# A decode kernel for two attentions: part of B's wo on eight DMA engines, wo rows permuted over partitions, finer last loads, x loaded first

## The chip, the cores and the metric

The kernel runs on one core of a Trainium2 chip. The metric is the device time in microseconds (us); the kernel before takes 254.8 us. The span of a profile is about 2 us shorter than that time.

In the profile lines, PE is TensorE (matmuls), DVE is VectorE, ACT is ScalarE, POOL is GpSimd and SP is SyncE, which issues the big loads; a q behind a name marks the engine's queue, and L500 is line 500 of that kernel. A semaphore is a counter on which engines wait.

## The reference, cut to what matters

Two independent attentions with one query row each, A over a window of the last 2048 cache rows, B over all 8192.

```python
D = 576; Hq, Hkv, Sk, Dh = 32, 16, 8192, 128        # bf16; wo: (Hq*Dh, D) = (4096, 576)
q = (x @ wq).reshape(1, 1, Hq, Dh)                  # for A and for B
k, v = k_cache[:, :, Sk - W:], v_cache[:, :, Sk - W:]   # A: W = 2048; B: all rows
p = softmax(q @ k^T * Dh**-0.5)                     # two query heads share one kv head
out = (p @ v).reshape(1, 1, Hq * Dh) @ wo           # (1, 1, 576) each, concatenated
```

Nothing is used twice, so some 103 MB have to be read once. Of these, the two wo matrices are 2 x 4096 x 576 x 2 B = 9.4 MB.

## The kernel before

All big loads come from one queue (SP) and go through six buffers (slots) of 128 partitions x 16 KB. The recording helper `add` lists operations with the resources that they read and write and makes the semaphore waits from that.

```python
    def load(src_of, view_of, what):
        s = slot_n[0] % NSLOT
        slot_n[0] += 1
        res = ("slot", s)
        add("sp", lambda sp: sp.dma_start(view_of(slots[:, s, :]), src_of()), writes=[res], dma="slot%d" % s)
        return s
    # ... (cut)
    def load_wo(P, k):                       # WO_SLOT = 14: three loads of 14, 14 and 4 rows per partition
        lo, hi = k * WO_SLOT, min(HQ, (k + 1) * WO_SLOT)
        return load(lambda: wos[P].rearrange("(p j) n -> p (j n)", p=128)[:, lo * DM:hi * DM],
                    lambda v: v[:, 0:(hi - lo) * DM], "wo")
```

Partition p holds rows 32p to 32p+31 of wo; "row 14" below means row 14 of these 32 on every partition. The attention result is brought into the same layout (`opj`) by matmuls with a 0/1 matrix `pick`; then each of the 32 rows takes four matmuls, one for each quarter of the 576 columns.

```python
    for j in range(4):
        add("pool", select(pick[:], -128 * j, [[1, 4], [-1, 128]], 4), reads=["pick"], writes=["pick"])
    # ... (cut)
    for jj in range(lo, hi):                 # in wo_part
        for j in range(4):
            o = (jj - lo) * DM + j * OUTW
            ins = pe.matmul(misc[32 * j:32 * j + 32, 0:OUTW], lhsT=opj[:, P, jj:jj + 32],
                            rhs=slots[:, s, o:o + OUTW], start=(jj == 0), stop=(jj == HQ - 1))
    # ... (cut) the end of the kernel
    for k in range(3):
        wo_part(0, k, load_wo(0, k))
    finish_out(0)
    vb1 = list(range(NS[1]))
    v_some(1, 1, vb1, NS[1])                 # the last eight V loads of B
    store_out(0)
    combine(1)
    for k in range(3):
        wo_part(1, k, load_wo(1, k))
    finish_out(1)
    store_out(1)
```

## Time and profile before

| what | before |
|---|---|
| time, median of 4 runs | 254.83 us |
| span of the profile | 252.8 us |
| DMA: mean rate over the span | 408 GB/s |
| last wo load landed, eight fastest engines / last engine | 242.8-244.1 / 249.3 us |
| matmuls left when B's second wo load had landed | 72, from 247.95 to 250.3 us |

The busy share in 40 slices (each 6.3 us, digits are tenths) and the rate of the DMA in each slice, kernel before:

```profile
DMA  7999999999999999999999999999999999999960
GB/s 283 398 440 430 433 415 428 433 417 425 432 423 423 430 423 423 433 421 423 430 417 436 425 415 436 430 412 441 421 421 419 430 425 425 428 423 429 425 284 31
```

The DMA engines are busy for nine tenths or more of every slice from the second to the 38th. The kernel is bound by the stream of loads.

The table of DMA queues before (queue, kind: packets, MB, share of the time of 16 engines):

```profile
q1 hardware_dynamic: 7504, 102.77, 96.1%
q8 instruction: 27, 0.44, 0.7%
```

The second line is the fetching of the program itself, in 27 packets of 16 KB.

The trace also records every increment of a semaphore by a DMA. A load of 128 partitions leaves 16 such landings, and the page counts 16 DMA engines, so each landing is read here as the end of that load on one engine. They are not a view of the profile page; here they are read from the trace, sorted by time within one load, in us from the start of the span:

```
before, the third K load of A: 28.6 to 29.1 on all sixteen
before, last load of B's wo (rows 28-31):
  242.83 242.84 242.90 243.00 243.05 243.43 243.71 244.14
  247.35 247.37 247.42 247.46 247.56 247.63 249.06 249.30
```

Sixteen engines that started together end in two groups of eight. The fast eight got a 2 MB load done every 4.89 us throughout. The others fell back in steps of about 1.45 us. There were 26 instruction fetches by then (a median of 1.07 us each); spread over eight engines in turn that would give six engines three and two engines four of them, which fits the two groups within the late eight. The trace fits it all the way: at the loads that landed first at 64, 128, 182 and 222 us, the late eight were 5, 13, 19 and 24 such steps behind in sum, and 5, 13, 19 and 24 fetches had begun. Below, "early" and "late" engines mean these.

The tail before, in order of time (start us, us, engine, line, operation, [idle before it and what ended that]):

```profile
243.44 1.87 PE L500 MATMUL misc<-slots,opj 128*32 128x144 bf16 x56 [0.37 <-DVE opj L491]
247.95 2.35 PE L500 MATMUL misc<-slots,opj 128*32 128x144 bf16 x72 [2.64 <-DMA slots<-in_B_wo_dram]
250.36 0.31 DVE L506 CAST outsb<-misc 128x144 bf16<-128x144 f32 x1 [7.06 <-PE misc L500]
250.69 0.58 SPq L512 DMA_DIRECT2D out_dram<-outsb  x1
```

PE does the first 14 rows (56 matmuls) at once, waits for the second load, and then has 72 matmuls left.

### The profile page before, as it was taken

The numbers are of one execution on the slowest core, as the hardware profiler recorded it, in microseconds if no ns is written. First come the engines' busy times: TensorE is split into PE (matmuls) and PEld (weight loads), VectorE is DVE, ScalarE is ACT, GpSimd is POOL, SyncE is SP. The second block draws the span as 40 slices with busy tenths as digits, with TensorE's granted clock in tenths as the row PEclk, the third lists the DMA queues.
The fourth block names the chain that finished last, engine by engine and source line by source line (L and its number), as shares of the span: only waits on it lengthen the run. The fifth ranks groups of instructions, "written<-read, shape, count | busy, mean of one in ns | idle before, by whom it ended". The sixth has DMA issues, their size and how long they took to land.

```text
span 252.8 us, 7319 instructions
## 1 busy us (share of the span) xinstructions
PE 167.1 (66%) x3438; PEld 131.7 (52%) x3438; DVE 79.3 (31%) x141; ACT 87.3 (35%) x92; POOL 22.4 (9%) x31
## 2 busy tenths in 40 slices
PE   0018999787799995888694994858943634332563
PEld 0003877456578874766474673655732633232453
DVE  0181545427544462357341340313425100000010
ACT  2000766445566683565461461423630000000000
POOL 8996000000000000000000000000000000000000
PEclk9999999999979999799997798968977665555555
DMA  7999999999999999999999999999999999999960
GB/s 283 398 440 430 433 415 428 433 417 425 432 423 423 430 423 423 433 421 423 430 417 436 425 415 436 430 412 441 421 421 419 430 425 425 428 423 429 425 284 31
DMA packets 7822, 103.24 MB, mean 408 GB/s; under 512 B 1136, under 2 KB 1136, under 8 KB 1648
## 3 DMA queue, kind: packets, MB, share of 16 engines
q1 hardware_dynamic: 7504, 102.77, 96.1%
q8 instruction: 27, 0.44, 0.7%
q10 hardware_dynamic: 288, 0.00, 0.1%
q14 instruction: 3, 0.02, 0.0%
HBM read 102.76 MB, written 0.00 MB: 407 GB/s over the span
## 4 chain that ended last, share of the span: by engine, by line
DMA 53%; PE 38%; DVE 6%; issue 1%; POOL 1%; ACT 0%; SPq 0%; POOLq 0%
DMA slots<-in_B_k_cache_dram 21%; PE ktps L339 20%; DMA slots<-in_B_v_cache_dram 17%; DMA slots<-in_B_wo_dram 11%; PE sacc L362 7%; DMA xtwo<-in_A_x_dram 4%; PE opsum L464 3%; DVE xpad L287 3%; PE opsum L302 2%; PE misc L302 2%; PE misc L500 2%; DVE ptm L407 1%; PE misc L396 1%; PE misc L444 1%; PE misc L431 0%
## 5 line engine op out<-in xcount | busy, mean ns | idle before, releaser
L345 ACT ACTIVATE kt<-ktps 128x1024 bf16<-128x1024 bf16 x80 | 78.0, 1023 | 65.3 <-PE ktps L339 65.1
L339 PE MATMUL ktps<-ident,slots 128*128 128x128 bf16 x1280 | 86.4, 231 | 19.1 <-DMA slots<-in_B_k_cache_dram 19.1
L339 PEld LDWEIGHTS ktps<-ident,slots 128*128 128x128 bf16 x1280 | 80.0, 105 | 31.5 <-DMA slots<-in_B_k_cache_dram 20.3
L348 DVE COPY kt<-ktps 128x1024 bf16<-128x1024 bf16 x80 | 55.3, 691 | 79.2 <-PE ktps L339 79.0
L464 PE MATMUL opsum<-slots,ptm 128*32 128x128 bf16 x1280 | 28.3, 256 | 29.4 <-DMA slots<-in_B_v_cache_dram 28.9
L464 PEld LDWEIGHTS opsum<-slots,ptm 128*32 128x32 bf16 x1280 | 24.5, 116 | 35.6 <-DMA slots<-in_B_v_cache_dram 33.0
L362 PE MATMUL sacc<-kt,qtm 128*32 128x512 bf16 (+1 forms) x384 | 30.1, 411 | 0.3 <-DVE kt L348 0.3
L302 PE MATMUL opsum<-slots,xpad 128*32 128x512 bf16 x72 | 8.7, 460 | 19.3 <-DVE xpad L287 19.3
L302 PEld LDWEIGHTS opsum<-slots,xpad 128*32 128x32 bf16 x72 | 2.5, 112 | 22.2 <-issue 21.3
L224 POOL MEMSET ptm<- 128x8192 uint32 x2 | 13.8, 6926 | 0.0
L478 DVE TENSOR_SCALAR acc<-opsum,stat 128x128 f32<-128x128 f32 x2 | 0.7, 346 | 39.6 <-PE opsum L464 39.6
L362 PEld LDWEIGHTS sacc<-kt,qtm 128*32 128x32 bf16 x384 | 7.0, 98 | 6.9 <-ACT kt L345 1.1
L500 PE MATMUL misc<-slots,opj 128*32 128x144 bf16 x256 | 8.1, 323 | 3.4 <-DMA slots<-in_B_wo_dram 2.6
L308 ACT ACTIVATE qrow<-opsum 128x512 bf16<-128x512 f32 x2 | 1.2, 597 | 24.1 <-PE misc L302 24.1
L500 PEld LDWEIGHTS misc<-slots,opj 128*32 128x32 bf16 x256 | 7.4, 146 | 3.8 <-DMA slots<-in_B_wo_dram 3.4
L287 DVE TENSOR_SCALAR xpad<-xtwo,par 128x5 bf16<-128x5 bf16 x4 | 6.4, 3098 | 8.3 <-DMA xtwo<-in_A_x_dram 8.3
L302 PE MATMUL misc<-slots,xpad 128*32 128x512 bf16 x72 | 8.5, 450 | 0.0
L385 ACT ACTIVATE psb<-sacc,stat 128x2048 bf16<-128x2048 f32 x3 | 5.9, 1967 | 7.5 <-DVE stat L379 7.5
L562 POOL MEMSET ptm<- 128x512 uint32 x1 | 0.5, 526 | 86.1 <-PE opsum L464 86.1
L407 DVE TENSOR_SCALAR ptm<-misc,par 128x256 bf16<-128x256 bf16 (+1 forms) x16 | 6.9, 526 | 3.7 <-PE misc L396 3.7
L396 PE MATMUL misc<-ident,psb 128*128 128x128 bf16 x48 | 4.1, 235 | 3.7 <-DVE ptm L407 3.7
L396 PEld LDWEIGHTS misc<-ident,psb 128*128 128x128 bf16 x48 | 3.0, 105 | 5.4 <-DVE ptm L407 4.3
(50 smaller groups left out, 37.2 us busy)
## 6 DMA issues: line engine op xcount, KB each, us to landing
slots<-in_B_k_cache_dram SPq DMA_DIRECT2D x16, 2048.0 KB, 22.3
slots<-in_B_v_cache_dram SPq DMA_DIRECT2D x16, 2048.0 KB, 25.1
slots<-in_A_k_cache_dram SPq DMA_DIRECT2D x4, 2048.0 KB, 19.3
slots<-in_A_v_cache_dram SPq DMA_DIRECT2D x4, 2048.0 KB, 20.7
slots<-in_A_wq_dram SPq DMA_DIRECT2D x2, 2048.0 KB, 9.6
slots<-in_B_wq_dram SPq DMA_DIRECT2D x2, 2048.0 KB, 18.6
slots<-in_A_wo_dram SPq DMA_DIRECT2D x2, 2016.0 KB, 25.0
slots<-in_B_wo_dram SPq DMA_DIRECT2D x2, 2016.0 KB, 28.7
```

What stands on the lines that cost most here:

```text
L224: add("pool", lambda pool, b=b: pool.memset(ptm[:, b, :].bitcast(U32), 0), writes=[("ptm", b)])
L287: add("dve", lambda dve, e=e: dve.tensor_scalar(xpad[:, P, 5 * e:5 * e + 5, 0], xtwo[:, P, 0:5], par[2][:, e:e + 1], None, ALU.mult), read ...
L302: ins = pe.matmul(qps[c][32 * j:32 * j + 32, :], lhsT=xpad[:, P, x, :], rhs=slots[:, s, o:o + 512], start=(u == 0), stop=(u == WQ_UNITS - 1))
L339: ins = pe.matmul(ktps_bf[q][:, t * 128:(t + 1) * 128], lhsT=slots[:, s, o:o + 128], rhs=ident[:, :], start=True, stop=True, is_transpose= ...
L345: add("act", lambda act, q=q, dst=dst: act.activation(dst, ktps_bf[q], ACT.Copy), reads=[("bank", q)], writes=[("kt", u, q)])
L348: add("dve", lambda dve, q=q, dst=dst: dve.tensor_copy(dst, ktps_bf[q]), reads=[("bank", q)], writes=[("kt", u, q)])
L362: ins = pe.matmul(sacc[32 * j:32 * j + 32, o:o + w], lhsT=qtm[:, P, g * 32:(g + 1) * 32], rhs=rhs, start=(g == 0 and o % 512 == 0), stop=( ...
L385: return act.activation(psb[:, 0:w * G[P]].rearrange("p (x g) -> p x g", g=G[P]), src, ACT.Exp, bias=st(P, C_NB + c), scale=SCALE, accum_o ...
L396: ins = pe.matmul(misc_bf[:, t * 128:(t + 1) * 128], lhsT=psb[:, o:o + 128], rhs=ident[:, :], start=True, stop=True, is_transpose=True)
L407: ins = dve.tensor_scalar(dst, src, par[G[P]][:, e:e + 1], None, ALU.mult)
L464: ins = pe.matmul(opsum[32 * j:32 * j + 32, 0:DH], lhsT=ptm[:, pb, o:o + 32], rhs=slots[:, s, b * 128:(b + 1) * 128], start=(i == 0 and u ...
L500: ins = pe.matmul(misc[32 * j:32 * j + 32, 0:OUTW], lhsT=opj[:, P, jj:jj + 32], rhs=slots[:, s, o:o + OUTW], start=(jj == 0), stop=(jj == ...
```

## The change

The intent was to let the eight early engines take over some of the late engines' load, to leave less PE work behind the last landing, and to start PE earlier. Rows 14-19 of B's wo go in two halves of 64 partitions, whose source pattern has an outermost dimension of 8. For that, the rows are permuted over the partitions (partition 8a+b holds row block a+16b), for A and B alike. The last four rows go in two loads of two. x is loaded first, and the memset of ptm (the buffer for the transposed softmax weights, cleared by POOL at the start) is cut into pieces. Two tiny probe loads were left in.

```diff
-        return load(lambda: wos[P].rearrange("(p j) n -> p (j n)", p=128)[:, lo * DM:hi * DM],
-                    lambda v: v[:, 0:(hi - lo) * DM], "wo")
+    def load_wo(P, parts):
# ... (cut)
+            for h in range(2 if halves else 1):
+                p0, pn = (64 * h, 64) if halves else (0, 128)
+                def go(sp, p0=p0, pn=pn, lo=lo, n=n, o=o):
+                    src = bass.AP(tensor=wo.tensor, offset=wo.offset + (p0 // 8) * HQ * DM + lo * DM,
+                                  ap=[[HQ * DM, pn // 8], [16 * HQ * DM, 8], [1, n]])
+                    return sp.dma_start(slots[p0:p0 + pn, s, o:o + n], src)
# ... (cut)
-        add("pool", select(pick[:], -128 * j, [[1, 4], [-1, 128]], 4), reads=["pick"], writes=["pick"])
+        add("pool", select(pick[:], -128 * j, [[1, 4], [-1, 16], [-16, 8]], 4), reads=["pick"], writes=["pick"])
# ... (cut)
-    for k in range(3):
-        wo_part(0, k, load_wo(0, k))
+    for parts in ([(0, 14, 0)], [(14, 28, 0)], [(28, 32, 0)]):
+        for made in load_wo(0, parts):
+            wo_part(0, *made)
# ... (cut) two probe loads of 8 and 12 partitions, 512 B each
-    for k in range(3):
-        wo_part(1, k, load_wo(1, k))
+    for parts in ([(0, 14, 0)], [(14, 20, 1), (20, 28, 0)], [(28, 30, 0), (30, 32, 0)]):
+        for made in load_wo(1, parts):
+            wo_part(1, *made)
# ... (cut) load_x(0), load_x(1) moved to the head of ACT's queue
-        add("pool", lambda pool, b=b: pool.memset(ptm[:, b, :].bitcast(U32), 0), writes=[("ptm", b)])
+        for h in range(8):
+            add("pool", lambda pool, b=b, h=h: pool.memset(ptm[:, b, h * 2048:(h + 1) * 2048].bitcast(U32), 0),
+                writes=[("ptm", b)])
```

More of the change, by code (lines that the diff above doesn't have):

```diff
@@ L24 @@
 WQ_SLOT = 4
-WO_SLOT = 14
 OUTW = DM // 4
@@ L51, in __init__, with add @@
         self.dma_count = {}
-    def add(self, eng, fn, reads=(), writes=(), dma=None):
+    def add(self, eng, fn, reads=(), writes=(), dma=None, after=()):
         op = Op(eng, fn, tuple(reads), tuple(writes), dma)
@@ L65, in add @@
                 deps.append((w, False))
+            deps += [(o, False) for o in self.readers.get(r, ())]
+        for r in after:
             deps += [(o, False) for o in self.readers.get(r, ())]
@@ L202, in bass_concat_heads__sliding_block_cached__gqa_block_cached__decode_kernel, with load_x, go @@
     B_M = ("bank", 7)
+    def load_x(P):
+        def go(act):
+            x = xs[P]
+            with nc.allow_non_contiguous_dma(reason="small x load"):
+                src = bass.AP(tensor=x.tensor, offset=x.offset, ap=[[9, 64], [4, 2], [1, 5]])
+                return act.dma_start(xtwo[:, P, 0:5], src)
+        add("act", go, writes=[("xtwo", P)], dma="x%d" % P)
+    load_x(0)
+    load_x(1)
     def setup(pool):
@@ L254, in load @@
         return s
-    def load_x(P):
-        def go(act):
-            x = xs[P]
-            with nc.allow_non_contiguous_dma(reason="small x load"):
-                src = bass.AP(tensor=x.tensor, offset=x.offset, ap=[[9, 64], [4, 2], [1, 5]])
-                return act.dma_start(xtwo[:, P, 0:5], src)
-        add("act", go, writes=[("xtwo", P)], dma="x%d" % P)
     def load_wq(P, k):
@@ L277, in load_kv @@
         return load(src, lambda v: v, "kv")
-    def load_wo(P, k):
-        lo, hi = k * WO_SLOT, min(HQ, (k + 1) * WO_SLOT)
-        return load(lambda: wos[P].rearrange("(p j) n -> p (j n)", p=128)[:, lo * DM:hi * DM],
-                    lambda v: v[:, 0:(hi - lo) * DM], "wo")
+    def load_wo(P, parts):
+        s = slot_n[0] % NSLOT
+        slot_n[0] += 1
+        wo = wos[P]
+        o, made = 0, []
+        for k, (lo, hi, halves) in enumerate(parts):
+            n = (hi - lo) * DM
+            res = ("slot", s) if len(parts) == 1 and not halves else ("slot", s, k)
+            for h in range(2 if halves else 1):
[4 more added lines that the diff above has]
+                    return sp.dma_start(slots[p0:p0 + pn, s, o:o + n], src)
+                add("sp", go, writes=[res + (h,) if halves else res], after=[("slot", s)],
+                    dma="slot%d" % s if res == ("slot", s) else "part%d_%d_%d" % (s, k, h))
+            made.append((lo, hi, s, o, [res + (h,) for h in range(2)] if halves else [res]))
+            o += n
+        return made
     def x_columns(P):
@@ L491, in combine, with wo_part @@
         add("dve", lambda dve: dve.tensor_copy(opj[:, P, 0:32], misc[:, 0:32]), reads=[B_M], writes=[("opj", P)])
-    def wo_part(P, k, s):
-        lo, hi = k * WO_SLOT, min(HQ, (k + 1) * WO_SLOT)
+    def wo_part(P, lo, hi, s, o0, res):
         def mm(pe):
@@ L498, in mm @@
                 for j in range(4):
-                    o = (jj - lo) * DM + j * OUTW
+                    o = o0 + (jj - lo) * DM + j * OUTW
                     ins = pe.matmul(misc[32 * j:32 * j + 32, 0:OUTW], lhsT=opj[:, P, jj:jj + 32],
@@ L502, in mm @@
             return ins
-        add("pe", mm, reads=[("opj", P), ("slot", s)], writes=[B_M])
+        add("pe", mm, reads=[("opj", P)] + res, writes=[B_M])
     def finish_out(P):
@@ L513, in store_out @@
         add("sp", put, reads=[("outsb", P)], writes=[("out", P)], dma="out%d" % P)
-    load_x(0)
-    load_x(1)
     def k_phase(P, c, between):
@@ L581, in bass_concat_heads__sliding_block_cached__gqa_block_cached__decode_kernel @@
     store_out(0)
+    probe = nc.alloc_sbuf_tensor("probe", [128, 512], BF16)
+    for k in (8, 12):
+        add("sp", lambda sp, k=k: sp.dma_start(probe[0:k, (k - 8) * 64:(k - 8) * 64 + 256], ks[0][0, 0, 0:2 * k, :].rearrange("(p t) d -> p (t d)", t=2)),
+            writes=["probe%d" % k], dma="probe%d" % k)
     combine(1)
-    for k in range(3):
-        wo_part(1, k, load_wo(1, k))
+    for parts in ([(0, 14, 0)], [(14, 20, 1), (20, 28, 0)], [(28, 30, 0), (30, 32, 0)]):
+        for made in load_wo(1, parts):
+            wo_part(1, *made)
     finish_out(1)
     store_out(1)
-    add("sp", lambda sp: sp.nop(), reads=[("out", 0), ("out", 1)])
+    add("sp", lambda sp: sp.nop(), reads=[("out", 0), ("out", 1), "probe8", "probe12"])
     prog.emit()
```

## The prediction

> **What bounds the kernel now.** The DMA stream: the slices show DMA at 9 tenths from the second to the 38th, 420-440 GB/s. The trace's semaphore landings (one per DMA engine and load) show more. On eight engines successive 2 MB loads land every 4.89 us from start to end without a gap (131 KB per engine: 26.8 KB/us). The other eight fall behind in steps of about 1.45 us: the spread within one load is 0.46 us at 29 us, 1.97 at 50, 3.5 at 100, 4.9 at 160, 6.5 at the end. The queue table has 27 instruction fetches of 16 KB, 1.0-1.1 us each, 26 of them before the stream ends: over eight engines that is six with three and two with four, just as the landings show.[...] The last wo load lands at 242.8-244.1 us on eight, 247.4-247.6 on six, 249.1-249.3 on two.
>
> The tail (timeline): 72 wo matmuls from 247.95 to 250.3 at a granted clock of 0.5, 33 ns each, then eviction and store until 252.8.
>
> **The change.**
> 1. Six of 32 rows of B's wo (885 KB) go in two 64-partition loads whose source has an outermost dimension of 8. [...]the four landings of A's 4-partition store came 0.2 us behind those of four *early* engines (232.0-233.3 us). So the late eight lose 55 KB each (-2.06 us), the early eight gain as much. Late: six at 245.4, two at 247.2; early 244.9-246.2.
> 2. The last two loads are 2 rows: 8 matmuls (0.3 us) follow the last landing. With rows 20-28 landing near 245.8, PE works almost without waits from 243.4 (opj ready, unchanged) for 128 x 33 ns = 4.2 us, ending near 247.7 instead of 250.3. PE and DMA end about together, so neither part alone gives all of it.
> 3. x first, ptm memsets in pieces: q starts at 18.0 us now, because x lands at 11.8 behind wq packets and the two xpad multiplications take 3.0 us each beside POOL's 6.9 us memsets. It should start near 8 us, and PE's backlog (the chain of waits shows it up to 98 us) goes. But the DMA rings never ran dry: worth 0 to 0.3 us.
> 4. Permuted rows: same packets; pick absorbs it: 0. Two probe loads and three more issues: [...]off the path.
>
> **Predicted.** 2.6 us less, all in the last 10 us: 254.8 -> 252.2 us, range 251.3 to 253.4 (1%). Faster by over 2% 0.03, within 2% 0.95, slower by over 2% 0.02.
>
> **What would show each step.** Landings of the last loads within about 2 us instead of 6.5; the halves landing on the early engines; last landing near 247.2; 8 matmuls after it. First q matmul near 8 us, xpad multiplications well under 3 us, the last V load landing when it does now. Still 26-27 fetches[...].
>
> **What would make it wrong.** If the 8 engines are the late ones, the last landing moves to 251.3 and the time to about 256.7. If smaller or far-apart packets run slower, or x ahead of wq delays the stream's start, up to 1 us of the gain goes. If opj comes later, PE sets the end. A fetch that falls on an engine after its data is through gains 1.4 us; one more during the last loads loses as much.

The ground on which step 1 took it that a load with 8 outermost runs on eight engines, and on which eight, is the four early landings of A's 4-partition store, so that the eight are the early ones stands there as the author's guess. -2.06 us is 55 KB at the measured 26.8 KB/us, PE ends near 247.7 instead of 250.3 us (2.6 us less), step 3 adds 0 to 0.3 us and step 4 nothing, so 254.8 becomes 252.2 us. The 1.4 us for a fetch is an estimate from the steps of 1.45 us.

## The result, and the profile after

The changed kernel takes 282.98 us (median of 4 runs, 282.55 to 283.84) against 254.83 (254.37 to 255.15): the ratio is 1.111, with a 95% interval of 1.108 to 1.115. A ratio here is the mean time of one kernel's fast runs over that of the other's in the same rounds, so it is not quite the ratio of the medians. The prediction was 252.2 us. It is wrong by 31 us, and in direction.

The same lines of the page after, with slices of 7.0 us, and the queues:

```profile
DMA  7999999999999999999999999999999999999950
GB/s 290 418 423 434 423 430 418 430 425 429 423 423 427 423 423 430 422 430 425 427 427 420 430 418 434 401 205 223 230 230 382 425 430 425 430 238 218 186 171 24
q1 hardware_dynamic: 7832, 102.78, 95.8%
q8 instruction: 27, 0.44, 0.6%
```

The DMA is as busy as before but moves half as much in two stretches: four slices from the 27th on, and the last slices from the 36th on. The stretches in between run at the old rate. A busy engine is not an engine at its rate; the GB/s row has to be read with the DMA row. The DMA issues (line engine op xcount, KB each, us from issue to landing) name what is in flight there; first before, then after:

```profile
slots<-in_A_wo_dram SPq DMA_DIRECT2D x2, 2016.0 KB, 25.0
slots<-in_B_wo_dram SPq DMA_DIRECT2D x2, 2016.0 KB, 28.7
```

```profile
slots<-in_A_wo_dram SPq DMA_DIRECT2D x2, 2016.0 KB, 37.3
slots<-in_B_wo_dram SPq DMA_DIRECT2D x1, 2016.0 KB, 38.2
```

A's wo, too, which the prediction had taken as unchanged, lands 12 us later after its issue. In the trace, the wo packets of 16128 B took a median of 604 ns before and 1175 ns after; the packets of 16384 B (wq, K and V) took 613 ns in both.

The main pieces of the chain that ended last, after, from 170 us on (start us, us, what; the prediction had expected no change before the last 10 us):

```profile
174.02 36.33 DMA slots<-in_A_wo_dram
210.39 1.90 PE misc L522 x29
212.35 24.96 DMA slots<-in_B_v_cache_dram
237.36 1.93 PE opsum L488 x64
239.90 37.34 DMA slots<-in_B_wo_dram
277.28 0.46 PE misc L522 x8
```

And the tail after, with the 8 matmuls behind the last landing that the change was to bring. They came, but 27 us late:

```profile
267.79 1.87 PE L522 MATMUL misc<-slots,opj 128*32 128x144 bf16 x56 [4.78 <-DMA slots<-in_B_wo_dram]
273.13 0.91 PE L522 MATMUL misc<-slots,opj 128*32 128x144 bf16 x24 [3.47 <-DMA slots<-in_B_wo_dram]
275.72 1.39 PE L522 MATMUL misc<-slots,opj 128*32 128x144 bf16 x40 [1.67 <-DMA slots<-in_B_wo_dram]
277.28 0.43 PE L522 MATMUL misc<-slots,opj 128*32 128x144 bf16 x8 [0.17 <-DMA slots<-in_B_wo_dram]
```

### The profile page after: what moved, and what is told of

The parts are those of the page before. It is cut to its first block, busy times and chain, and to the rows that moved or that the text cites. A ratio compares the mean times of both kernels' runs of the same rounds, so it can differ in the third digit from the quotient of the medians.

```text
span 280.6 us, 7338 instructions
## 1 busy us (share of the span) xinstructions
PE 169.1 (60%) x3438; PEld 132.5 (47%) x3438; DVE 81.1 (29%) x141; ACT 87.4 (31%) x92; POOL 24.7 (9%) x45
## 4 chain that ended last, share of the span: by engine, by line
DMA 64%; PE 29%; DVE 5%; issue 1%; ACT 0%; SPq 0%
DMA slots<-in_B_k_cache_dram 25%; PE ktps L363 17%; DMA slots<-in_B_wo_dram 13%; DMA slots<-in_A_wo_dram 13%; DMA slots<-in_B_v_cache_dram 9%; PE sacc L386 5%; DMA xtwo<-in_A_x_dram 4%; DVE xpad L311 3%; PE opsum L326 2%; PE misc L326 2%; PE opsum L488 1%; PE misc L522 1%; DVE ptm L431 0%; PE misc L420 0%; DVE stat L401 0%
## 5 line engine op out<-in xcount | busy, mean ns | idle before, releaser
L488 PE MATMUL opsum<-slots,ptm 128*32 128x128 bf16 x1280 | 29.1, 261 | 41.1 <-DMA slots<-in_B_v_cache_dram 40.7
L488 PEld LDWEIGHTS opsum<-slots,ptm 128*32 128x32 bf16 x1280 | 25.4, 118 | 47.2 <-DMA slots<-in_B_v_cache_dram 44.7
L522 PE MATMUL misc<-slots,opj 128*32 128x144 bf16 x256 | 9.0, 324 | 16.7 <-DMA slots<-in_B_wo_dram 10.1
L238 POOL MEMSET ptm<- 128x1024 uint32 x16 | 14.3, 951 | 0.0
L311 DVE TENSOR_SCALAR xpad<-xtwo,par 128x5 bf16<-128x5 bf16 x4 | 8.1, 3957 | 7.1 <-DMA xtwo<-in_A_x_dram 7.1
L528 DVE CAST outsb<-misc 128x144 bf16<-128x144 f32 x2 | 0.6, 308 | 25.2 <-PE misc L522 25.2
## 6 DMA issues: line engine op xcount, KB each, us to landing
slots<-in_B_v_cache_dram SPq DMA_DIRECT2D x16, 2048.0 KB, 28.2
```

What stands on the lines that cost most here:

```text
L238: add("pool", lambda pool, b=b, h=h: pool.memset(ptm[:, b, h * 2048:(h + 1) * 2048].bitcast(U32), 0), writes=[("ptm", b)])
L311: add("dve", lambda dve, e=e: dve.tensor_scalar(xpad[:, P, 5 * e:5 * e + 5, 0], xtwo[:, P, 0:5], par[2][:, e:e + 1], None, ALU.mult), read ...
L488: ins = pe.matmul(opsum[32 * j:32 * j + 32, 0:DH], lhsT=ptm[:, pb, o:o + 32], rhs=slots[:, s, b * 128:(b + 1) * 128], start=(i == 0 and u ...
```

## The experiments

### Why are permuted rows slow?

The permutation changes two things at once: the addresses (neighbouring partitions now hold rows 590 KB apart) and the shape of the source pattern (16 outermost, then 8). Two theories follow.

- Address theory: HBM delivers rows that far apart slowly.
- Port theory: what counts is which partitions the sixteen engines write at one time, not the addresses. Why, and which sets of partitions get in each other's way, was a supposition that no view and no run shows. It is left out here and cut from the expectations; there, "port theory" stands for the numbers that it foretold.

Over how many engines a load is spread shows in its landings. In the changed kernel, a load with 16 outermost left 16 and each half, with 8 outermost, left 8 (one increment soon after the issue not counted); a load of k partitions, up to 16, left k (e4_map, below). No view shows which engine writes which partition.

**e1_far16**: the kernel before with the permuted source pattern and the permuted `pick`, nothing else.

```diff
-        return load(lambda: wos[P].rearrange("(p j) n -> p (j n)", p=128)[:, lo * DM:hi * DM],
+        wo = wos[P]
+        return load(lambda: bass.AP(tensor=wo.tensor, offset=wo.offset + lo * DM,
+                                    ap=[[HQ * DM, 16], [16 * HQ * DM, 8]] + [[1, (hi - lo) * DM]]),
-        add("pool", select(pick[:], -128 * j, [[1, 4], [-1, 128]], 4), reads=["pick"], writes=["pick"])
+        add("pool", select(pick[:], -128 * j, [[1, 4], [-1, 16], [-16, 8]], 4), reads=["pick"], writes=["pick"])
```

> The kernel before, with nothing changed but the source pattern of the wo loads (16 rows outermost, then 8 rows 590 KB apart, as in the changed kernel) and the selector that undoes the permutation. All theories that put the loss on the permuted wo loads: the wo packets of 16128 B take about 1.2 us instead of 0.60, each 9.4 MB of the two wo matrices costs about twice its 22 us, the time is 270 to 280 us. If it stays near 254.8 us, the permutation is innocent and the halves or the probes are to blame.

Measured: 280.88 us against 254.71 for the kernel before on the same chip (one run each). So the permutation alone costs 26.2 us, nearly all of the 28.2 us. Packets of 16128 B took 1169 ns instead of 604. The mean granted TensorE clock is lower here and in the changed kernel (0.79 against 0.84 before), but from 20 to 98 us the clock (0.98) and the DMA's rate (425 GB/s) are those of the kernel before; the loss begins with the wo loads, for which PE waits, so the clock is not its cause.

**e2_near16** (the diff is against e1_far16, and the old `pick` is back): the old row order, but 16 outermost. Without more, the two dimensions would describe the same rows as one of 128, so the outer step is 512 B short; the result is wrong.

```diff
-                                    ap=[[HQ * DM, 16], [16 * HQ * DM, 8]] + [[1, (hi - lo) * DM]]),
+                                    ap=[[8 * HQ * DM - 256, 16], [HQ * DM, 8]] + [[1, (hi - lo) * DM]]),
```

> The kernel before, wo rows in their old order but with a source pattern whose outermost dimension is 16 (its step is shortened by 512 B so that the two dimensions do not merge into 128; the result is therefore wrong on purpose). Port theory[...]: as slow as the permuted rows, packets of 16128 B near 1.2 us, 270 to 280 us. Address theory (rows 590 KB apart are read slowly from HBM): as fast as before, packets near 0.60 us, 254 to 256 us.

Measured: 279.71 us, packets of 16128 B at 1168 ns. Near addresses are as slow as far ones.

**e3_far32** (the diff is against e1_far16; `pick` is permuted to match): the rows permuted even further apart (1180 KB), but with 32 outermost.

```diff
-                                    ap=[[HQ * DM, 16], [16 * HQ * DM, 8]] + [[1, (hi - lo) * DM]]),
+                                    ap=[[HQ * DM, 32], [32 * HQ * DM, 4]] + [[1, (hi - lo) * DM]]),
```

> The kernel before, wo rows permuted with 32 outermost and 4 rows 1180 KB apart inside; the selector undoes it, the result is right. Port theory[...]: as fast as before, packets of 16128 B near 0.60 us, 254 to 256 us. Address theory (far apart rows are slow): slow, packets clearly above 0.8 us, above 262 us.

Measured: 254.70 us against 254.71, right result, packets at 604 ns. Far addresses cost nothing.

The rate of the DMA per slice of e1_far16, e2_near16 and e3_far32, in this order:

```profile
GB/s 291 404 433 432 428 421 428 418 432 422 423 432 418 435 418 428 422 432 423 421 432 421 428 430 421 434 217 223 229 223 342 428 428 425 428 278 211 213 186 46
```

```profile
GB/s 283 404 443 417 441 417 424 429 417 433 427 424 422 424 429 422 426 427 429 422 422 434 417 427 432 420 248 220 224 234 337 427 422 429 429 308 212 213 198 43
```

```profile
GB/s 275 399 428 425 441 417 424 433 417 430 426 422 425 422 430 422 425 431 420 428 425 428 425 420 430 430 420 433 421 421 424 430 425 422 428 428 426 422 288 41
```

The two kernels with 16 outermost show the two holes of the changed kernel, the one with 32 has none. The address theory has fallen.

**e5_halves64** tells the partitions from a cost of the pattern itself: each wo load is cut into two plain two-dimensional loads of 64 partitions, in the old row order, on 16 engines.

```diff
+        if what == "wo":
+            for h in range(2):
+                add("sp", lambda sp, h=h: sp.dma_start(view_of(slots[64 * h:64 * h + 64, s, :]), src_of()[64 * h:64 * h + 64, :]),
+                    writes=[res] if h == 0 else [("half", s)], dma="slot%d" % s if h == 0 else "half%d" % s)
+            return s
# ... (cut) the matmuls wait for both halves
```

> The kernel before, each wo load cut into two plain loads of 64 partitions (rows in their old order, 16 engines each, no third dimension). Port theory: [...]16128 B packets near 1.17 us, 276 to 281 us, like the permuted rows. Rival (an outermost dimension of 16 before an inner one is slow in itself[...]): packets near 0.60 us, 254 to 257 us.

Measured: 280.85 us (one run), packets of 16128 B at 1180 ns, and the same two holes in the rate:

```profile
GB/s 298 394 435 432 425 427 413 434 420 433 420 425 423 430 423 434 415 425 430 423 432 420 425 423 434 421 242 180 213 239 351 425 430 420 430 309 218 216 168 38
```

Without any odd pattern, 64 partitions at a time run at half the rate. So it takes no odd shape to lose this much. What these loads have in common with those of 16 outermost no view shows; the port theory had foretold both. At 16128 B in 1169 ns (e1_far16) an engine moved 13.8 B/ns, at 604 ns (e3_far32 and before) 26.7 B/ns (1 B/ns is 1 GB/s). From 180 to 212 us all of them together moved 235 GB/s in e1_far16, 238 in e2_near16 and 230 in e5_halves64, against 426 in e3_far32.

Where the 26 us of e1_far16 go can be read from its trace: the time of all packets of one size, summed and divided by the sixteen engines, is 18.7 us more than before for the packets of the two wo, and 7.0 us more for those of 16384 B. That is 25.7 us together. So V loads next to the wo loads suffer as well; the spread between the engines within a load rises from 5 to 11-13 us there.

### Which engines are the early ones?

**e4_map**: the kernel before with 16 tiny loads, of 1 to 16 partitions, behind A's store.

```diff
+    for k in range(1, 17):
+        add("sp", lambda sp, k=k: sp.dma_start(probe[0:k, (k - 1) * 192:k * 192], bass.AP(tensor=ks[0].tensor, offset=ks[0].offset, ap=[[256, k], [1, 192]])),
+            writes=["probe%d" % k], dma="probe%d" % k)
# ... (cut) the last wait of the kernel includes the probes
```

> The kernel before with 16 tiny loads of 1 to 16 partitions behind the store of A, to see by their landings which of the DMA engines are the early ones and which the late ones. Step 1 of the prediction[...]: the loads of 2 to 8 partitions land on early engines only, each partition above 8 adds a late landing. The probes of the changed kernel speak against it (8 partitions: six early and two late landings; 12: seven and five): then one or two of the first eight land late. Time 254.5 to 256 us.

Measured: 255.91 us (one run). A load of k partitions left k landings (for k below 16 also one increment 0.4 to 0.6 us after the issue, left out here), and each one more than the load before. The trace does not number the engines. Here and in the expectations, engine k-1 is the one whose landing the load of k partitions adds to those of the load before; that the others are the same engines each time is taken from their early and late landings, which stay as they were:

```
partitions   5: 232.51 232.64 232.96 233.41 233.55
partitions   6: 232.68 232.83 233.14 233.59 233.73 236.66
partitions   7: 232.85 233.01 233.31 233.76 233.91 236.85 237.47
partitions   8: 232.49 233.02 233.20 233.49 233.93 234.08 237.05 237.66
partitions   9: 232.72 232.73 233.21 233.39 233.68 234.11 234.28 237.31 237.88
partitions 10-15: one late landing more each (7 early and 3, 4, ... 8 late)
partitions  16: 8 early, 8 late
```

So engines 0 to 4, 7, 8 and 15 are early, 5, 6 and 9 to 14 are late. Of the eight that the change gives more work, two are late ones. The prediction had seen only that the first four are early and had gone on to eight. In the changed kernel the probe of 8 partitions had also left six early and two late landings.

### Would the idea work with the permutation mended?

**e6_quarters**: the changed kernel with the fast permutation (32 outermost), and rows 14-19 of B in four loads of 32 partitions with 8 outermost, meant for engines 0 to 7 (the halves of the changed kernel, also with 8 outermost, left 8 landings).

```diff
-                                  ap=[[HQ * DM, pn // 8], [16 * HQ * DM, 8], [1, n]])
+                                  ap=[[R, an], [32 * R, 4], [1, n]])      # R = HQ*DM; an = 8 for a quarter, 32 else
# ... (cut) the loop over the parts of a load; `pick` permuted as in e3_far32
-    for parts in ([(0, 14, 0)], [(14, 20, 1), (20, 28, 0)], [(28, 30, 0), (30, 32, 0)]):
+    for parts in ([(0, 14, 32)], [(14, 20, 8), (20, 28, 32)], [(28, 30, 32), (30, 32, 32)]):
```

> The changed kernel with its fault mended: wo permuted with 32 outermost (fast in e3_far32), the six rows in four loads of 32 partitions on 8 engines[...]. Both theories: the 23 us are gone. Engine theory of the prediction (what counts is each engine's own queue), with the map of e4_map (late engines are 5, 6 and 9 to 14): engines 5 and 6 end 2.1 us later than the late ones of before (about 249.5 us), 9 to 14 2.1 us earlier (about 245.5). Port theory[...]: engines 9 to 14 are no earlier[...]; last landing 249.5 us or later. Time 254.0 to 256.5 us under both; the landings tell them apart.

Measured: 259.68 us, ratio 1.0196 (1.0182 to 1.0210). The 23 us are gone, but the time is 3.2 us above the expected range: B's last load landed on its last engine at 254.6 us, 5.3 us later than before. No late engine was relieved: apart from two (242.7 and 243.2 us), all landings of that load lie between 249.0 and 254.6 us. The engine theory wanted six engines near 245.5.

**e7_five** (the diff is against e6_quarters): as e6_quarters, but four rows, in loads of 20 partitions with 5 outermost, meant for engines 0 to 4 only, early ones all (the load of 5 partitions in e4_map left 5 early landings, 232.5 to 233.6 us).

```diff
-    for parts in ([(0, 14, 32)], [(14, 20, 8), (20, 28, 32)], [(28, 30, 32), (30, 32, 32)]):
+    for parts in ([(0, 14, 32)], [(14, 18, 5), (18, 28, 32)], [(28, 30, 32), (30, 32, 32)]):
```

> As e6_quarters, but four rows of B's wo in loads of 20 partitions, which use only engines 0 to 4, early ones all. Engine theory: late engines end 1.4 us earlier than before (six near 246.1, two near 247.8), engines 0 to 4 2.8 to 3.4 us later (246 to 247.5); with 2-row last loads the kernel ends 1.5 us earlier: 253.0 to 253.6 us. Port theory: [...]late landings stay within 0.4 us of before (247.5 and 249.3) or the early engines take over their lateness; 254.2 to 255 us.

Measured: 256.73 us, ratio 1.0078 (1.0065 to 1.0092). The last landing is at 251.2 us. Here the engines, by the map of e4_map, were the right ones, and the late engines still ended later instead of 1.4 us earlier. The time is worse than the port theory's number as well.

**e8_straight**: the changed kernel without the permutation and without the eight-engine loads.

```diff
-                                  ap=[[HQ * DM, pn // 8], [16 * HQ * DM, 8], [1, n]])
+                                  ap=[[HQ * DM, 128], [1, n]])
-        add("pool", select(pick[:], -128 * j, [[1, 4], [-1, 16], [-16, 8]], 4), reads=["pick"], writes=["pick"])
+        add("pool", select(pick[:], -128 * j, [[1, 4], [-1, 128]], 4), reads=["pick"], writes=["pick"])
-    for parts in ([(0, 14, 0)], [(14, 20, 1), (20, 28, 0)], [(28, 30, 0), (30, 32, 0)]):
+    for parts in ([(0, 14, 0)], [(14, 20, 0), (20, 28, 0)], [(28, 30, 0), (30, 32, 0)]):
```

> The changed kernel without the permutation and without the eight-engine loads: rows 14-20, 20-28, 28-30, 30-32 of B's wo in plain 128-partition loads; x first, memsets in pieces and probes kept. Last landing as before (249.3 us); after rows 20-28 land (247.9) 32 + 8 matmuls of 33 ns follow instead of 72, and 8 after the last landing: span 0.7 us shorter, 253.9 to 254.4 us. If x first were worth anything it would be below 253.9.

Measured: 254.66 us, ratio 0.9999 (0.9986 to 1.0013). The last landing is at 249.29 us, as before; the store of B starts at 250.15 instead of 250.69 us, but the span ends only 0.2 us earlier.

**e9_ownports** is the control for e7_five, and the diff is against that. Sources, packet sizes and engines are the same; only the destination differs: engines 0 to 4 write their extra rows into partitions 0-19 and 32-51, which the author took for partitions that they write anyway (most of the rows go into a spare buffer, `kt`, on these partitions). The result is wrong.

```diff
-                    return sp.dma_start(slots[4 * a0:4 * (a0 + an), s, o:o + n], src)
+                    dst = slots[4 * a0:4 * (a0 + an), s, o:o + n]
+                    if cut == 5:
+                        p0 = 32 * (h % 2)
+                        dst = slots[p0:p0 + 4 * an, s, o:o + n] if h < 2 else kt[p0:p0 + 4 * an, h // 2 - 1, 0:n]
+                    return sp.dma_start(dst, src)
# ... (cut) these loads also wait until `kt` is free
```

> As e7_five with the same sources, packets and engines, but engines 0 to 4 write their extra rows into partitions 0-19 and 32-51 only[...], partly into a spare buffer; so the result is wrong on purpose. Port theory: [...]last landings come 1.4 us before those of before (six near 246.1, two near 247.9, instead of 249 to 251 in e7_five), the time is 253.0 to 253.7 us. Rival (few-partition loads or small packets slow the late engines[...]): like e7_five, 256.2 to 257 us.

Measured: 253.24 us against 254.53, ratio 0.9950 (0.9934 to 0.9965). It lies where the port theory put it. The landings of B's last load (rows 30-31) in both:

```
e7_five:     244.78 244.95 245.03 249.10 249.35 249.57 249.65 249.74 249.84 249.88 250.10 250.13 250.43 250.53 251.16 251.18
e9_ownports: 241.73 241.89 241.98 246.22 246.24 246.25 246.35 246.54 246.66 246.69 246.73 246.94 247.34 247.40 247.80 247.88
```

And the last matmuls, which follow them, first of e7_five, then of e9_ownports:

```profile
249.87 1.87 PE L524 MATMUL misc<-slots,opj 128*32 128x144 bf16 x56 [1.10 <-DMA slots<-in_B_wo_dram]
```

```profile
246.51 1.87 PE L528 MATMUL misc<-slots,opj 128*32 128x144 bf16 x56 [0.89 <-DMA slots<-in_B_wo_dram]
```

Same bytes on the same five engines, and 3.3 us between them, by the destination partitions. The packets show the loss itself: from 237 to 244 us those of 16128 B, most of them on the other engines, took a median of 1095 ns in e7_five and 606 ns in e9_ownports. Over the whole stream, the packets' time divided by sixteen engines was 246.0 us in e7_five and 242.7 us in e9_ownports, again 3.3 us apart (e6_quarters: 246.7; the kernel before: 242.5). So what the early engines took over had to go to other partitions too, or nothing was won here. Before, the last landing was at 249.3 us; here it is at 247.9.

### The other parts of the change

**e10_xfast**: the kernel before with x first and the ptm memsets moved behind the xpad multiplications.

```diff
+    load_x(0)                                  # now ahead of everything on ACT's queue
+    load_x(1)
-    for b in range(2):
-        add("pool", lambda pool, b=b: pool.memset(ptm[:, b, :].bitcast(U32), 0), writes=[("ptm", b)])
+        if P == 0:                             # in q_phase, after x_columns
+            for b in range(2):
+                add("pool", lambda pool, b=b: pool.memset(ptm[:, b, :].bitcast(U32), 0), reads=[("xpad", 0)], writes=[("ptm", b)])
```

> The kernel before with x loaded first and the big ptm memsets moved behind the xpad multiplications (whole, not in pieces). Step 3 of the prediction, in the form that the changed kernel did not reach: q starts near 11.5 us instead of 18, xpad multiplications take 0.3 us, PE's backlog goes early; and the time stays within 0.3 us of before (254.4 to 255.0), because the DMA rings never ran dry. Rival: the backlog counted, and up to 6 us are gained.

Measured: 254.90 us against 254.53, ratio 1.0011 (0.9999 to 1.0024). The xpad multiplications, as a group (line engine op, xcount | busy, mean ns | idle before), of the kernel before, the changed kernel and e10_xfast:

```profile
L287 DVE TENSOR_SCALAR xpad<-xtwo,par 128x5 bf16<-128x5 bf16 x4 | 6.4, 3098 | 8.3 <-DMA xtwo<-in_A_x_dram 8.3
```

```profile
L311 DVE TENSOR_SCALAR xpad<-xtwo,par 128x5 bf16<-128x5 bf16 x4 | 8.1, 3957 | 7.1 <-DMA xtwo<-in_A_x_dram 7.1
```

```profile
L289 DVE TENSOR_SCALAR xpad<-xtwo,par 128x5 bf16<-128x5 bf16 x4 | 0.7, 230 | 7.1 <-DMA xtwo<-in_A_x_dram 7.1
```

The xpad multiplications bring x into the layout from which q is made. Cutting the memset into 16 pieces of 951 ns did not let the multiplications in between; in both kernels they ended 0.94 us after the last piece of ptm, and q started at 18.57 us instead of 18.00. With the memsets out of the way a multiplication took 0.23 us and q started at 11.1 us. The seven microseconds gained by PE are worth nothing at the end of the kernel.

**e11_tail**: the kernel before with only B's last wo loads cut finer.

```diff
-    for k in range(3):
-        wo_part(1, k, load_wo(1, k))
+    for parts in ([(0, 14)], [(14, 22), (22, 28)], [(28, 30), (30, 32)]):
+        for made in load_wo(1, parts):
+            wo_part(1, *made)
```

> The kernel before with only B's last wo loads cut finer: rows 14-22, 22-28, 28-30, 30-32 in plain 128-partition loads, no probes. Last landing 249.3 us as before; 24 + 8 matmuls follow the landing of row 28, 8 the last one; the store starts at 250.0 to 250.2 instead of 250.7 us; 254.0 to 254.5 us. If e8_straight lost its tail gain to the two probes' waits at the end, this is 0.3 us faster than e8_straight; if the time stays at 254.7, the tail was not on the path.

Measured: 254.14 us against 254.53, ratio 0.9989 (0.9976 to 1.0001). Its last matmuls and its store:

```profile
249.43 0.43 PE L505 MATMUL misc<-slots,opj 128*32 128x144 bf16 x8 [0.26 <-DMA slots<-in_B_wo_dram]
250.25 0.57 SPq L517 DMA_DIRECT2D out_dram<-outsb  x1
```

That is about the 0.4 us that the trace shows (the store starts at 250.25 instead of 250.69), but the interval still holds 1. Its end behind the store is 0.4 us shorter than that of e8_straight, which waits for the probes there; whether the waits cost that was not tried by itself.

### A version that beats both

**e12_move** moves bytes to other partitions, with a right result. It is e11_tail, and the last four rows of A's wo lie on partitions 0-19, 28-31, 32-51 and 60-63 only, twelve columns instead of four. Partitions 0-19 and 32-51 are those of e9_ownports; that 28-31 and 60-63 do as well is supposition and was not tried by itself. A is taken because PE has slack there (before, it was busy for 15.6 of the 32 us from 180 to 212 us). A second selector `pickx` brings A's attention result into that layout.

```diff
+        for h in range(6):      # blocks a+32b, a = 5h..5h+4, on partitions 32*(h%2) + 4*(a-5h) + b, column group h//2
+            put(h, 32 * (h % 2), 20, h // 2, 5 * h, [[R, 5], [32 * R, 4]])
+        for e in range(2):      # blocks 30+e+32b on partitions 32e+28+b
+            put(6 + e, 32 * e + 28, 4, 0, 30 + e, [[32 * R, 4]])
# ... (cut) twelve matmuls with pickx, a copy to opx, then for the 12 columns:
+                    ins = pe.matmul(misc[32 * j:32 * j + 32, 0:OUTW], lhsT=opx[:, i:i + 32],
+                                    rhs=slots[:, s, o:o + OUTW], start=(i == 0), stop=False)
```

> A kernel with right results that uses what the experiments showed: e11_tail, and the last four rows of A's wo (not B's, because PE has slack there) are laid on partitions 0-19, 28-31, 32-51 and 60-63 alone, in loads that run on engines 0 to 4 for the most part[...]; twelve more selector matmuls and 32 more wo matmuls pay for it. Port theory: [...]B's last landing comes 1.4 us before that of e11_tail (248.0 instead of 249.4), the time is 252.6 to 253.2 us. If the extra PE work or the few-partition loads in the middle of the stream hold up the V loads[...], it is 254 us or more.

Measured: 253.27 us (252.93 to 253.32) against 254.98 (254.51 to 255.19) for the kernel before on the same chip; ratio 0.9930 (0.9916 to 0.9943). Each of its runs was below each run of the kernel before. B's last landing is at 248.57 us: 0.8 us before that of e11_tail, not the 1.4 expected, so the median is just above the expected range. Its last matmuls, to be set beside those of e11_tail:

```profile
248.61 0.43 PE L559 MATMUL misc<-slots,opj 128*32 128x144 bf16 x8 [0.51 <-DMA slots<-in_B_wo_dram]
```

Part of the rest is in slower packets: their time divided by sixteen engines is 0.4 us more than in e11_tail (243.1 against 242.7 us). Which packets was not looked into. At 0.7% it is the fastest kernel with a right result here.

## Why the prediction was wrong, point by point

1. **"Permuted rows: same packets; pick absorbs it: 0."** This is the step that failed. It looked at packet sizes and at the matmuls and did not ask what else changes in a load once its outermost dimension is 16. It cost 26.2 us (e1_far16). The prediction's own list of risks has "far-apart packets run slower", at up to 1 us; the runs show that distance costs nothing (e3_far32) and that 16 outermost costs as much without it (e2_near16). What the runs showed in its place: with 16 outermost (the changed kernel, e1_far16, e2_near16) or 64 partitions at a time (e5_halves64) the packets of 16128 B take 1168 to 1180 ns instead of 604, as the port theory foretold for e2_near16 and e5_halves64, and with 32 outermost they take 604 (e3_far32). That the destination partitions decide is shown by e9_ownports against e7_five (606 against 1095 ns); for 16 outermost and for the halves it was not shown, since no view tells which engine writes which partition.
2. **"So the late eight lose 55 KB each (-2.06 us), the early eight gain as much."** This failed twice. Engines 5 and 6 are late ones (e4_map); four landings of a 4-partition store were stretched to eight. And the step counted the bytes of each engine, where their destination counted too: with loads on early engines only, the late ones still ended later (e7_five), and earlier only when the bytes went to partitions 0-19 and 32-51 (e9_ownports, 1.4 us earlier than before). e7_five lost 2 us and e6_quarters 5 us, more than the port theory had foretold (254.2 to 255 and 254.0 to 256.5 us). The traces show more for e7_five: the packets of 16128 B themselves were slower while the extra loads ran (1095 against 606 ns), so the extra loads cost time and did not only fail to save it.
3. **"8 matmuls (0.3 us) follow the last landing."** The mechanism held: 8 matmuls in 0.43 us came last. By itself it moved the start of the store by 0.44 us (e11_tail), since the last landing stayed at 249.3-249.4 us; the 2.6 us needed the part that failed.
4. **"q ... should start near 8 us"** was wrong: 18.57 us. x landed at 10.7 instead of 11.8 (the packets of the two x ran from 5.4 to 13.4 us, among those of wq), and beside the memset in pieces the two multiplications took 7.8 us. But **"the DMA rings never ran dry: worth 0 to 0.3 us"** held: with q really early (11.1 us) the time did not fall (e10_xfast).
5. **Two probe loads and more issues: off the path.** Without permutation and eight-engine loads, everything else of the change together came to a ratio of 0.9999 (e8_straight).
6. **Still 26-27 fetches**: 27. That they make the late engines late fits in number, in the steps and in their times, but no run changed the fetches, so it is argued and not shown.

The chance of 0.02 for "slower by over 2%" was much too low for a change that rewrote the pattern of 9% of the bytes of a kernel bound by DMA.

## What to carry to other kernels

In a kernel bound by loads, ask of every changed load how long its outermost dimension is and which partitions it writes at one time, not only how many bytes and packets it has: with 16 outermost, or with 64 partitions, sixteen busy engines here delivered half (230 to 238 against 426 GB/s). Work that was moved from late engines to early ones had to go to other partitions as well here (e9_ownports against e7_five: 3.3 us), by another layout; the matmul behind it can pay for that where PE has slack. When a rate halves under a busy share of 9 tenths, compare the time of single packets of the same size: it showed at once which loads were slow (1175 against 604 ns at 16128 B, 613 ns in both at 16384 B).
